# A whole-program order list for a recurrent attention and MLP kernel, and rings of four tiles

## The chip, the cores and the metric

The kernel runs on one NeuronCore of a Trainium2 chip. The metric is device time in microseconds (us) of one execution; the time of a kernel is the median of its runs. A profiled execution has a time of its own and a span, which runs from the first instruction to the end of the last one.

## The reference, cut to what matters

For four batches, eight heads and 768 tokens of head size 48, a recurrent attention gives `y`; the 3072 rows of 384 numbers then go through two matrix products with a leaky ReLU (slope 0.01) between them.

```
for t in range(S):
    cur = einsum('bhd,bhe->bhde', u * k[t], v[t])
    y[t] = einsum('bhd,bhde->bhe', r[t], state + cur)
    state = w * state + einsum('bhd,bhe->bhde', k[t], v[t])
x = y as rows of H * D = 384
h = x @ w_in                 # 384 -> 2048
out = maximum(0.01 * h, h) @ w_out   # 2048 -> 384
```

Inputs and output are float32; the kernel computes mostly in bfloat16.

## The kernel before, in words

The tokens are cut into 24 **stages** of 128 tokens: stage n is chunk n // 4 of batch n % 4, so stage n + 4 goes on from the state that stage n leaves. Each stage is a small chain over five engines, and each step of it has a letter that the program's order list uses, with the stage's number behind it:

- `k`, `r`, `v`: loads of the stage's rows, float32 to bfloat16, as DMAs issued by GpSimd (line 220; 1024 pieces of 192 bytes each). `wi` and `wo` (lines 230 and 234) load quarters of the two weight matrices in the same queue.
- `P` (DVE, line 361): k or r times a table of decay powers. `T` and `t` turn the product so that the head's dimension lies on partitions, by TensorE and a copy (stages 0 to 5); `XT` does the same by a DMA transpose that SyncE issues (line 366, stages 6 to 23).
- `A` (TensorE, line 453): scores of the stage, two PSUM banks. `q` (DVE, lines 390, 392 and 394): row sums of r u k. `Q` (GpSimd, line 401, two instructions): a tile with these sums on its diagonal. `M` (DVE, line 466, two halves `a` and `b`): writes the scores above the diagonal into that tile. Stages 0 to 3 take another way round for the diagonal (`X`, `D`, `Q` on DVE, line 462 for the mask).
- `Y` (TensorE, lines 585 and 592): scores times v plus r times the state. `y` (ScalarE, line 606): copies the result to `xT`.
- `K` (TensorE, line 494) and `S` (DVE, lines 560 and 562, or 557): the new state.
- `G` and `g` (lines 631 and 641): the first product of one stage and a group of 512 of the 2048 columns, and its leaky ReLU on ScalarE into `gT`. `J` and `j` (lines 654 and 664): the same for a pair of stages and 256 columns. A `J` is six matmuls of 256 columns, a `G` twelve of 128.
- `H` and `h` (lines 678 and 690): the second product of one stage, 16 matmuls of 384 columns, its copy and the store, which SyncE issues (line 692).
- `F` with a number: that many matmuls whose results nobody reads.

Every step is recorded by `add` (line 53) with what it reads and writes; each engine then plays its steps strictly in the recorded order, with semaphore waits worked out from the reads and writes. PSUM's eight banks are given out in recorded order too (`take`, line 192). So the order of recording is the order of each engine's queue, and a step that waits holds everything behind it on its engine.

Before, two things set that order. The text `ORDER` (lines 27 to 37) lists the start of the program up to the first matmuls of pair 3. Then a loop (lines 733 to 767) records pair after pair, for m from 3 to 11: the eight `J` of the pair, the scores and masks of the next pair, the preparation (`P`, `XT`) of the pair after, the loads of the one after that, row sums and diagonal tiles, and between them the two `H` of the previous pair and the `Y`, `K` and `S` of the next pair. Up to m = 5 (`LATE`) the scores stand behind the eight `J`; from m = 6 they stand behind the third. Loads in the loop wait for a `J` of the same turn (`pace`, line 753). `xT` and `gT` are rings of three buffers of 256 tokens (line 144).

Of the kernel before, what the change touches and what calls it, by code (L numbers as in the profile page):

```python
# [126 lines left out]
def bass_rwkv5_eagle__then__act_leaky_relu_kernel(  # L127
# [16 lines left out]
    NQK, NTP, NVS, NAT, NT, NX, NG, NO = 6, 6, 6, 6, 10, 3, 3, 4  # L144
# [477 lines left out]
    def g1(n, grp):  # L622
        ps_g, key = g_bank[n, grp] = take()
        m, half = divmod(n, 2)
        ix, t = m % NX, slice(128 * half, 128 * half + 128)

        def emit():
            for f in range(4):
                fb = 4 * grp + f
                for s in range(NSL):  # L630
                    last = PE.matmul(ps_g[:, 128 * f:128 * f + 128], w_in_sb[:, s, 128 * fb:128 * fb + 128],  # L631
                                     xT[ix][:, s, t], start=s == 0, stop=s == NSL - 1)
# [12 lines left out]

    def g1_pair(m, j):
        ps_g, key = g_bank[m, j, 2] = take()
        ix = m % NX

        def emit():  # L650
            for f in range(2):
                fb = 2 * j + f
                for s in range(NSL):
                    last = PE.matmul(ps_g[:, 256 * f:256 * f + 256], w_in_sb[:, s, 128 * fb:128 * fb + 128],  # L654
                                     xT[ix][:, s, :], start=s == 0, stop=s == NSL - 1)
            return last

        add("pe", emit, R=[("xT", ix, 0), ("xT", ix, 1), ("win", j // 2)],
            W=[key, ("pace", 2 * m, j), ("pace", 2 * m + 1, j)])
# [11 lines left out]
    def g2(n, c0=0, c1=HD):  # L671
        ps_o, key = o_bank[n, c0] = take()
        m, half = divmod(n, 2)
        ig = m % NG

        def emit():
            for s in range(NFB):
                last = PE.matmul(ps_o[:, 0:c1 - c0], gT[ig][:, s, 128 * half:128 * half + 128], w_out_sb[:, s, c0:c1],  # L678
                                 start=s == 0, stop=s == NFB - 1)
# [47 lines left out]
    for name in ORDER.split():  # L727
        if name in single:
            single[name]()
        else:  # L730
            what, n, rest = re.match(r"([A-Za-z]+?)(\d+)(.*)$", name).groups()
            stage[what](int(n), rest)
    for m in range(FIRST // 2, NST // 2):
        due, ahead, far = ([n for n in (2 * m + x, 2 * m + x + 1) if n < NST] for x in (2, 4, 6))
        late = m < FIRST // 2 + LATE
        for j in range(8):
            if j == VISIT and not late:
                for n in due:
                    a_mm(n)
            g1_pair(m, j)  # L740
            g1_pair_out(m, j)
        for n in due if late else ():
            a_mm(n)
        if not late:
            for n in ahead:
                prep(n)
        for n in due:
            a_mask(n)
        if late:
            for n in ahead:  # L750
                prep(n)
        for n in far:
            load_stage(n, pace=[("pace", 2 * m, 1)])
        for n in ahead:
            row_sums(n)
            diag_tile(n)
        g2(2 * m - 2)
        g2_out(2 * m - 2)
        for n in due:
            y_part(n)  # L760
        turning = [n for n in due if n < NST - NB]
        for n in turning:
            kv_mm(n)
        for n in turning:
            state(n)
# [64 lines left out]
```

## Time and profile before

| | us |
|---|---|
| median of three runs (lowest, highest) | 169.99 (169.92, 170.53) |
| profiled execution, its time | 170.09 |
| profiled execution, its span | 168.3 |
| TensorE busy in the span | 161.6 |
| GpSimd busy | 111.1 |
| DVE busy | 110.2 |
| ScalarE busy | 91.0 |

The span is 1.79 us shorter than the time of the same execution. Busy times of an engine overlap with those of the others. A matmul's shown duration includes its passage through the array, so of two that follow each other the distance of their starts, and not the duration, is what one costs.

### The profile page before, as it was taken

The numbers are of one execution on the slowest core, as the hardware profiler recorded it, in microseconds if no ns is written. First come the engines' busy times: TensorE is split into PE (matmuls) and PEld (weight loads), VectorE is DVE, ScalarE is ACT, GpSimd is POOL, SyncE is SP. The second block draws the span as 40 slices with busy tenths as digits, with TensorE's granted clock in tenths as the row PEclk, the third lists the DMA queues.
The fourth block names the chain that finished last, engine by engine and source line by source line (L and its number), as shares of the span: only waits on it lengthen the run. The fifth ranks groups of instructions, "written<-read, shape, count | busy, mean of one in ns | idle before, by whom it ended". The sixth has DMA issues, their size and how long they took to land.

```text
span 168.3 us, 4915 instructions
## 1 busy us (share of the span) xinstructions
PE 161.6 (96%) x2116; PEld 122.6 (73%) x2116; DVE 110.2 (66%) x221; ACT 91.0 (54%) x168; POOL 111.1 (66%) x125
## 2 busy tenths in 40 slices
PE   5889979999999999999999999999999999999994
PEld 5767869986568768768668768768678678668663
DVE  7499978828992497497599998996996805000000
ACT  4658777892228537537436536537537447449221
POOL 7999996999699929939939976975960540000000
PEclk9999999999999999999999999999999999999999
DMA  7999999999999996995994995994999111011012
GB/s 108 105 157 162 171 192 167 150 170 155 150 230 150 118 95 186 80 126 156 90 147 129 125 162 142 153 97 113 146 104 143 32 47 51 0 51 47 29 65 95
DMA packets 101263, 20.18 MB, mean 120 GB/s; under 512 B 94457, under 2 KB 101242, under 8 KB 101242
## 3 DMA queue, kind: packets, MB, share of 16 engines
q0 software_dynamic: 76512, 10.03, 93.3%
q1 hardware_dynamic: 23690, 9.64, 28.1%
q8 instruction: 16, 0.26, 0.7%
q10 hardware_dynamic: 1040, 0.20, 0.6%
q14 instruction: 5, 0.04, 0.1%
HBM read 20.45 MB, written 4.72 MB: 150 GB/s over the span
## 4 chain that ended last, share of the span: by engine, by line
PE 69%; POOL 12%; DMA 9%; DVE 7%; issue 1%; ACT 0%; POOLq 0%; DVEq 0%
PE ps L678 31%; PE ps L654 29%; DMA k_sb<-in_k_dram 5%; PE ps L592 5%; DMA r_sb<-in_r_dram 4%; POOL r_sb L220 3%; DVE qk L361 3%; PE ps L453 3%; POOL k_sb L220 3%; POOL v_sb L220 2%; PE ps L494 2%; DVE at L466 1%; POOL at L401 1%; POOL w_in_sb L230 1%; DVE rku L392 1%; DVE ku L390 1%
## 5 line engine op out<-in xcount | busy, mean ns | idle before, releaser
L678 PE MATMUL ps<-w_out_sb,gT 128*128 128x384 bf16 (+2 forms) x400 | 65.6, 320 | 0.0
L401 POOL TENSOR_TENSOR at<-ident,s_tok 128x512 bf16<-128x512 bf16 x40 | 42.8, 1101 | 21.0 <-DVE s_tok L394 21.0
L654 PE MATMUL ps<-xT,w_in_sb 128*128 128x256 bf16 x480 | 54.9, 273 | 0.0
L678 PEld LDWEIGHTS ps<-w_out_sb,gT 128*128 128x128 bf16 x400 | 37.7, 98 | 22.4
L664 ACT ACTIVATE gT<-ps 128x512 bf16<-128x512 f32 x80 | 47.8, 597 | 8.7 <-PE ps L654 4.0
L654 PEld LDWEIGHTS ps<-xT,w_in_sb 128*128 128x128 bf16 x480 | 46.4, 98 | 6.7
L690 ACT ACTIVATE out_sb<-ps 128x384 f32<-128x384 f32 (+2 forms) x25 | 12.0, 479 | 55.8 <-PE ps L678 55.8
L466 DVE CAST_PREDICATED at<-mask,ps 128x512 bf16<-128x512 uint16 x40 | 25.0, 684 | 21.8 <-PE ps L453 21.8
L220 POOL DMA_DIRECT2D k_sb<-in_k_dram x23 | 21.1, 923 | 3.3 <-PE ps L654 3.3
L220 POOL DMA_DIRECT2D v_sb<-in_v_dram x24 | 22.2, 925 | 0.8 <-POOLq L815 0.8
L220 POOL DMA_DIRECT2D r_sb<-in_r_dram x23 | 21.0, 914 | 0.0
L392 DVE TENSOR_TENSOR rku<-r_sb,ku 128x384 bf16<-128x384 bf16 x20 | 17.8, 892 | 0.7
L631 PE MATMUL ps<-xT,w_in_sb 128*128 128x128 bf16 x192 | 12.6, 219 | 0.5 <-DMA w_in_sb<-in_moe_w_in_dram 0.5
L606 ACT ACTIVATE xT<-ps 128x384 bf16<-128x384 f32 x24 | 10.9, 491 | 2.3 <-PE ps L592 2.2
L361 DVE TENSOR_TENSOR qk<-r_sb,qtab 128x384 bf16<-128x384 bf16 x23 | 9.1, 400 | 4.5 <-DMA r_sb<-in_r_dram 4.1
L631 PEld LDWEIGHTS ps<-xT,w_in_sb 128*128 128x128 bf16 x192 | 10.9, 98 | 1.3 <-DMA w_in_sb<-in_moe_w_in_dram 0.7
L394 DVE TENSOR_REDUCE s_tok<-rku 128x8 f32<-128x384 bf16 x20 | 11.1, 553 | 0.7
L641 ACT ACTIVATE gT<-ps 128x512 bf16<-128x512 f32 x16 | 9.5, 599 | 3.4 <-PE ps L631 2.9
L562 DVE TENSOR_TENSOR st<-sum_t,wl 128x384 bf16<-128x384 bf16 x16 | 10.7, 672 | 0.5
L592 PE MATMUL ps<-at,v_sb 128*32 128x128 bf16 x384 | 10.7, 219 | 0.0
L361 DVE TENSOR_TENSOR qk<-k_sb,ktab 128x384 bf16<-128x384 bf16 x23 | 9.9, 434 | 0.7 <-DMA k_sb<-in_k_dram 0.7
L592 PEld LDWEIGHTS ps<-tp,st 128*32 128x32 bf16 x240 | 7.2, 96 | 3.1 <-issue 2.5
(64 smaller groups left out, 120.9 us busy)
## 6 DMA issues: line engine op xcount, KB each, us to landing
out_dram<-out_sb SPq DMA_DIRECT2D x23, 192.0 KB, 2.2
v_sb<-in_v_dram POOLq DMA_DIRECT2D x24, 96.0 KB, 5.3
r_sb<-in_r_dram POOLq DMA_DIRECT2D x23, 96.0 KB, 5.4
k_sb<-in_k_dram POOLq DMA_DIRECT2D x23, 96.0 KB, 5.1
w_in_sb<-in_moe_w_in_dram POOLq DMA_DIRECT2D x4, 384.0 KB, 7.0
w_out_sb<-in_moe_w_out_dram POOLq DMA_DIRECT2D x4, 384.0 KB, 8.5
tp<-qk SPq DMA_TRANSPOSE x18, 4.1
k_f<-in_k_dram ACTq DMA_DIRECT2D x1, 192.0 KB, 2.8
```

The lines of the kernel that those rows point to most:

```text
L220: add("pool", lambda: G.dma_start(dst, src), R=pace, W=[(which, n)], dma=f"{which}{n}")
L361: add("dve", lambda: V.tensor_tensor(qk[iq][:, H * half:H * half + H, 0:D], hd(src), hd(tab[:, :]), ALU.mult), R=[(name, n), "qk"[half] + ...
L392: add("dve", lambda: V.tensor_tensor(rku[i2][:, :], r_of(n), ku[i2][:, :], ALU.mult), R=[("r", n), ("ku", i2)], W=[("rku", i2)])
L394: add("dve", lambda: V.tensor_reduce(s_tok[i2][:, :], hd(rku[i2][:, :]), AX.X, ALU.add), R=[("rku", i2)], W=[("s", i2)])
L401: add("pool", lambda hh=hh, s_of=s_of: G.tensor_tensor(at[ia][:, hh, :, :], ident[:, :].unsqueeze(1).to_broadcast([128, NP, 128]), s_of.un ...
L466: add("dve", lambda: V.copy_predicated(at[n % NAT][:, hh, :, :], mask[:, :].bitcast(mybir.dt.uint16).unsqueeze(1).to_broadcast([128, NP, 1 ...
L592: last = PE.matmul(ps_y[32 * q:32 * q + 32, 128 * s:128 * s + 128], a, m, start=not whole and step == 0, stop=step == len(columns[q]) - 1)
L631: last = PE.matmul(ps_g[:, 128 * f:128 * f + 128], w_in_sb[:, s, 128 * fb:128 * fb + 128], xT[ix][:, s, t], start=s == 0, stop=s == NSL - 1)
L654: last = PE.matmul(ps_g[:, 256 * f:256 * f + 256], w_in_sb[:, s, 128 * fb:128 * fb + 128], xT[ix][:, s, :], start=s == 0, stop=s == NSL - 1)
L664: add("act", lambda: A.activation(gT[ig][:, 2 * j:2 * j + 2, :].rearrange("p f t -> p (f t)"), ps_g[:, :], AF.Prelu, alpha=0.01), R=[key], ...
L678: last = PE.matmul(ps_o[:, 0:c1 - c0], gT[ig][:, s, 128 * half:128 * half + 128], w_out_sb[:, s, c0:c1], start=s == 0, stop=s == NFB - 1)
L690: add("act", lambda: A.activation(out_sb[io][:, c0:c1], ps_o[:, 0:c1 - c0], AF.Copy), R=[key], W=held)
```

## The change

The loop goes. `ORDER` now lists the whole program, stage by stage and engine by engine, in an order that no longer repeats from pair to pair; only the two halves of the last `H` are recorded after it. Every step is there that was there before; the matmuls of `F` come to 49 where they were 55. The loads no longer carry `pace`: their places in GpSimd's queue alone hold them back. `G` and `J` are now one function with a width of one or two stages (a width of four, `Z`, is defined and not used). `xT` and `gT` become rings of two buffers of 512 tokens, so that a place is used again eight stages later instead of six. Below, the new list is cut to the stretches of which the text speaks.

```diff
-FIRST, NB, PACE = 6, B, 3
-TURNED, DIAG, CARRY, EXACT, RAW, VISIT, LATE = 6, 4, 4, 1, 1, 3, 3
+NB = B
+TURNED, DIAG, CARRY, EXACT, RAW = 6, 4, 4, 1, 1
 ORDER = """
-w8 k0 r0 u8 u v0z v0 ones table v0y tcol trow r2 tri id wlz id8 k2 zr F18 Cw c0k Wl wi1 F4 T0k qk0 E r5 c0q F10 T0q wu8
-k1 F1 TQ t0k r1 TK t0q qtab Cu ktab P2q v2 F3 A0 X0 W C P2k T2q k3 M0a D0 T2k t2q Q0 v1 t2k M0b F16 A2 r3 X2 Y0 P1k M2a
-wi3 D2 y0 T1k P1q M2b v3 t1k F3 T1q K2 u16 Q2 G0.1 k5 S2 t1q Y2 g0.1 P3k k4 X1 A1 y2 P5q K1 P3q D1 T3k wi2 M1a T5q t3k
-T3q U t5q@ r4 t3q G2.1 Q1 utab A3 wi0 X3 g2.1 G0.3 M1b wo0 M3b D3 K3 g0.3 Y1 v5 M3a G2.3 y1 Q3 k6 G1.3 P4k g2.3 q5 k7
-Y3 g1.3 T4k y3 v4 G1.1 t4k S3 G3.2 wo1 g1.1 P4q P5k G3.1 Q5 g3.2 S1 T5k g3.1 T4q G3.3 q4 t4q G0.0 t5k r6 g3.3 A4 A5
-g0.0 P0k G3.0 Q4 M5a K0 G1.2 g3.0 M5b S0 K5 G2.2 g1.2 wo3 G2.0 M4a g2.2 wo2 P7k G1.0 g2.0 P6k M4b r7 K4 Y5 g1.0 S4 Y4
-r9 y5 G0.2 S5 y4 k9 J2.7 g0.2 q6 r8 J2.5 j2.7 J2.6 k8 j2.5 J2.4 P6q j2.6 Q6 J2.0 X6T j2.4 J2.1 j2.0 J2.2 j2.1 k10 H2
-j2.2 P7q q7 v6 X7T v7 P9q v8 H3 P9k h2 q9 X9T Q7 P8q H1 h3 Q9 q8 v9 P8k A6 h1 X8T A7 M6b H0 Q8 M6a M7b M7a v11 K7 Y6 h0
-r10 S7 Y7 y6 K6 k11 y7 J2.3 S6 v10 j2.3 r11
+w8 wlz qk0 r0 trow ones F21 k0 table c0k wi1 c0q tcol tri zr id8 Cw F12 k2 id T0k u8 u v0y T0q r2 r1 wu8 v0z Wl E u16
+t0k Cu k1 TQ v0 TK r3 C k3 ktab t0q A0 qtab U utab P2k X0 M0a T2k t2k v2 P2q P1q D0 F4 T2q t2q F12 P1k k5 T1k T1q A2
+t1k wi0 M0b v1 Q0 Y0 P3q X2 D2 t1q A1 M2b T3q P3k T3k M2a y0 G0.1 X1 D1 Q2 Y2 t3q t3k A3 g0.1 W P5k P0k K0 M1a M1b wi2
+T5k Q1 G0.0 S0 y2 G2.0 r5 Y1 y1 M3b v3 K1 S1 g2.0 G2.1 v5 G2.2 g2.1 g2.2 G1.0 g1.0 g0.0 X3 G1.1 g1.1 k4 t5k M3a D3 P5q
+G1.2 r4 wi3 q5 G0.2 Q3 v4 Y3 y3 T5q K5 g1.2 k7 wo3 P4k T4k t4k q4 P4q G3.1 S5 T4q G3.2 wo2 Q5 g0.2 t4q G2.3 g3.1 t5q@
+g2.3 A4 A5 M5a G3.0 r7 Q4 M4a M4b G0.3 g0.3 G3.3 g3.2 K4 wo0 Y4 y4 M5b Y5 G1.3 P7k y5 J2.2 j2.2 J2.7 g3.0 j2.7 q7 K3 S3
+K2 wo1 J2.4 J2.6 S4 r6 k6 S2 P7q X7T r9 k9 P6q P6k r8 J2.0 J2.3 g3.3 q6 P8q v7 q9 r11 k8 j2.3 J2.5 j2.6 j2.4 H0 H3 g1.3
+X6T H2 k11 v6 P9q j2.0 k10 A7 v9 j2.5 A6 Q7 v8 M7a H1 Q6 M6a M6b Y6 M7b r10 P8k y6 r12 P10k P9k v11 q11 Y7 y7 X9T Q9
+q10 h1 h2 J2.1 j2.1 K7 k13 K6 S6 Q10 J3.0 q8 Q8 Q11 P12q v20 P11k h0 J3.5 j3.5 H4 P11q J3.1 j3.1 K8 v12 P10q J3.4 j3.4
+j3.0 X8T H5 v10 S8 S7 A9 M9b r15 X10T X11T A8 h4 h5 J3.2 J3.3 j3.3 J3.7 j3.2 M8a M8b M9a Y8 Y9 A10 A11 k12 y8 M10a M10b
...
+j5.5 J5.0 K13 j5.0 H7 h7 j4.5 P14q k18 P16q P14k j4.2 r20 q12 J5.2 j5.2 J5.7 H6 P17q X12T j4.3 X14T S13 H9 A13 j5.7 A12
+P16k k17 v14 Q13 P17k K14 X17T h6 j5.3 H8 q17 Q14 q15 M13b X16T h9 P15k J5.1 r19 r18 M13a P19k j5.1 P18k Q12 M12a Y13
+M12b P20q y13 Q15 X15T Y12 A14 Q17 q16 M14b v16 P19q X19T r22 A17 y12 J5.6 P18q X18T J6.7 j5.6 v15 r21 J6.0 M14a j6.0
+h8 q19 H10 j6.7 M17a J6.6 S14 q18 A15 Q16 A16 H11 M15a v21 M16b K16 M17b j6.6 M16a M15b k22 K15 h10 Q18 S15 Y17 h11 y17
+Y15 y15 P22q Y14 Y16 S16 A18 M18b y14 A19 J7.2 k20 P22k y16 J8.3 j8.3 J8.4 j8.4 J8.1 J6.2 j6.2 j8.1 J7.0 J7.1 J6.1 J6.3
...
 """
@@
-    NQK, NTP, NVS, NAT, NT, NX, NG, NO = 6, 6, 6, 6, 10, 3, 3, 4
+    NQK, NTP, NVS, NAT, NT, NX, NG, NO = 6, 6, 6, 6, 10, 2, 2, 4
@@
-    xT = [SB(f"xT{i}", [128, NSL, 256]) for i in range(NX)]
-    gT = [SB(f"gT{i}", [128, NFB, 256]) for i in range(NG)]
+    xT = [SB(f"xT{i}", [128, NSL, 512]) for i in range(NX)]
+    gT = [SB(f"gT{i}", [128, NFB, 512]) for i in range(NG)]
@@
-        m, half = divmod(n, 2)
+        ix, slot = n // 4 % NX, n % 4
@@
+    def g1_wide(n0, width, fb0, count):
+        ps_g, key = g_bank[n0, width, fb0] = take()
+        ix, slots = n0 // 4 % NX, range(n0 % 4, n0 % 4 + width)
+        t, step = slice(128 * slots[0], 128 * slots[0] + 128 * width), 128 * width
+
+        def emit():
+            for f in range(count):
+                fb = fb0 + f
                 for s in range(NSL):
+                    last = PE.matmul(ps_g[:, step * f:step * f + step], w_in_sb[:, s, 128 * fb:128 * fb + 128],
                                      xT[ix][:, s, t], start=s == 0, stop=s == NSL - 1)
             return last
@@
-        "G": lambda n, x: g1(n, int(x[1:])), "g": lambda n, x: g1_out(n, int(x[1:])),
-        "J": lambda n, x: g1_pair(n, int(x[1:])), "j": lambda n, x: g1_pair_out(n, int(x[1:])),
+        "G": lambda n, x: g1_wide(n, 1, 4 * int(x[1:]), 4), "g": lambda n, x: g1_wide_out(n, 1, 4 * int(x[1:]), 4),
+        "J": lambda n, x: g1_wide(2 * n, 2, 2 * int(x[1:]), 2), "j": lambda n, x: g1_wide_out(2 * n, 2, 2 * int(x[1:]), 2),
@@
-    for m in range(FIRST // 2, NST // 2):
-        due, ahead, far = ([n for n in (2 * m + x, 2 * m + x + 1) if n < NST] for x in (2, 4, 6))
...
-        g2(2 * m - 1)
-        g2_out(2 * m - 1)
-    g2(NST - 2)
-    g2_out(NST - 2)
+    run(ORDER)
     for c0, c1 in ((0, 256), (256, HD)):
         g2(NST - 1, c0, c1)
         g2_out(NST - 1, c0, c1)
```

More of the change, by code (lines that the diff above doesn't have):

```diff
@@ L646, in g1_pair @@
[L646 to L659, printed above, removed]
@@ L672, in g2 @@
         ps_o, key = o_bank[n, c0] = take()
-        m, half = divmod(n, 2)
-        ig = m % NG
+        ig, slot = n // 4 % NG, n % 4
         def emit():
             for s in range(NFB):
-                last = PE.matmul(ps_o[:, 0:c1 - c0], gT[ig][:, s, 128 * half:128 * half + 128], w_out_sb[:, s, c0:c1],
+                last = PE.matmul(ps_o[:, 0:c1 - c0], gT[ig][:, s, 128 * slot:128 * slot + 128], w_out_sb[:, s, c0:c1],
                                  start=s == 0, stop=s == NFB - 1)
             return last
-        add("pe", emit, R=[("gT", ig, half, j) for j in range(8)] + [("wout", i) for i in range(4)], W=[key])
+        add("pe", emit, R=[("gT", ig, slot, fb) for fb in range(NFB)] + [("wout", i) for i in range(4)], W=[key])
     def g2_out(n, c0=0, c1=HD):
@@ L726, in bass_rwkv5_eagle__then__act_leaky_relu_kernel, with run @@
     }
[L727 to L732, printed above, removed]
-    for m in range(FIRST // 2, NST // 2):
-        due, ahead, far = ([n for n in (2 * m + x, 2 * m + x + 1) if n < NST] for x in (2, 4, 6))
[L735 to L765, printed above, removed]
-        g2(2 * m - 1)
-        g2_out(2 * m - 1)
-    g2(NST - 2)
-    g2_out(NST - 2)
+    def run(names):
+        for name in names.split():
+            if name in single:
+                single[name]()
+            else:
+                what, n, rest = re.match(r"([A-Za-z]+?)(\d+)(.*)$", name).groups()
+                stage[what](int(n), rest)
+    run(ORDER)
     for c0, c1 in ((0, 256), (256, HD)):
```

47 lines of the change are left out of this document (22 added, 25 removed).

## The prediction

> **What bounds the kernel now.** I read the page first, then TensorE's timeline, then the waits, then the timelines of the engines that feed TensorE.
>
> ```profile
> span 168.3 us, 4915 instructions
> PE 161.6 (96%) x2116; PEld 122.6 (73%) x2116; DVE 110.2 (66%) x221; ACT 91.0 (54%) x168; POOL 111.1 (66%) x125
> PE   5889979999999999999999999999999999999994
> ```
>
> TensorE (PE) is busy for 96% of the span, and from the eighth of the 40 slices, some 30 us in, every slice but the last shows a 9. DVE and GpSimd (POOL) are busy for two thirds each. So a new order can save time in the first 30 us alone, and can lose it anywhere. TensorE's timeline gives its prices and the size of the start.
>
> ```profile
> 4.57 0.63 PE L424 MATMUL ps<-ident,raw 128*128 128x128 bf16 x4
> ...
> 29.14 2.17 PE L631 MATMUL ps<-xT,w_in_sb 128*128 128x128 bf16 x36
> 31.15 0.33 PE L494 MATMUL ps<-v_sb,qk 128*128 128x96 bf16 x4
> ...
> 32.99 4.75 PE L654 MATMUL ps<-xT,w_in_sb 128*128 128x256 bf16 x42
> 37.57 7.96 PE L678 MATMUL ps<-w_out_sb,gT 128*128 128x384 bf16 x48
> 45.47 0.82 PE L453 MATMUL ps<-tp 48*128 48x128 bf16 x16
> 46.22 2.77 PE L678 MATMUL ps<-w_out_sb,gT 128*128 128x384 bf16 x16
> ...
> 50.59 6.06 PE L654 MATMUL ps<-xT,w_in_sb 128*128 128x256 bf16 x54
> ...
> 63.69 5.40 PE L654 MATMUL ps<-xT,w_in_sb 128*128 128x256 bf16 x48
> 69.02 0.62 PE L453 MATMUL ps<-tp 48*128 48x128 bf16 x16
> 69.58 2.77 PE L678 MATMUL ps<-w_out_sb,gT 128*128 128x384 bf16 x16
> 72.28 0.24 PE L592 MATMUL ps<-tp,st 128*32 128x128 bf16 x4
> ...
> 73.18 0.51 PE L494 MATMUL ps<-v_sb,qk 128*128 128x96 bf16 x8
> 73.53 2.76 PE L678 MATMUL ps<-w_out_sb,gT 128*128 128x384 bf16 x16
> 76.13 5.40 PE L654 MATMUL ps<-xT,w_in_sb 128*128 128x256 bf16 x48
> ```
>
> From start to start: a G costs 0.67 us ((31.15 - 29.14) / 3), a J 0.67 ((69.02 - 63.69) / 8), an A 0.28 (0.56 / 2), an H 2.63 ((45.47 - 37.57) / 3), a Y 0.45 (0.90 / 2), a K 0.18 (0.35 / 2). A turn of the loop, 63.69 to 76.13, is 12.44 us without a gap. Against that, what stands from 4.57 to 37.57 (16 G, 7 J, six each of A, Y and K, twelve T and small things) comes to some 26 us by such prices and took 33: 7 us of waits and fills.
>
> What keeps the loop free of gaps is slack on the other engines, which the list of waits shows:
>
> ```profile
> DVE at L466 <- PE ps L453: 21.8, 8, 6.4
> POOL at L401 <- DVE s_tok L394: 21.0, 9, 6.5
> ```
>
> DVE waits 21.8 us in all for scores (A), GpSimd 21.0 us for row sums. Both stand ready before TensorE needs them.
>
> **Part 1: the start.** Early on, GpSimd's queue and the transfers set the pace. These are GpSimd's rows around the first two diagonal tiles (Q5, Q4) and behind them, two DMA rows from the chain of waits, the weights' row of the page, and the landing times of the 18 transposes (line 366).
>
> ```profile
> 22.32 2.13 POOL L401 TENSOR_TENSOR at<-ident,s_tok 128x512 bf16<-128x512 bf16 x2
> ...
> 26.75 2.28 POOL L401 TENSOR_TENSOR at<-ident,s_tok 128x512 bf16<-128x512 bf16 x2 [1.47 <-DVE s_tok L394]
> 28.98 1.56 POOL L234 DMA_DIRECT2D w_out_sb<-in_moe_w_out_dram  x2
> 30.53 1.78 POOL L220 DMA_DIRECT2D r_sb<-in_r_dram  x2
> ...
> 15.61 7.52 DMA r_sb<-in_r_dram
> 32.27 8.17 DMA k_sb<-in_k_dram
> w_in_sb<-in_moe_w_in_dram POOLq DMA_DIRECT2D x4, 384.0 KB, 7.0
> DMA to landing us min/median/max: 2.7/4.1/7.4
> ```
>
> r4, issued at 15.61, lands at 23.12; its row sums follow, Q4 starts 1.47 us late and ends at 29.03. Then come two weight quarters and r7, issued at 30.53 and landed near 38.5 (by the 7.5 and 8.2 of the two DMA rows); its transpose takes some 7 us under such load (the 7.4), and the A of stages 6 and 7 stand at 45.47. So that A is Q4's end plus 16.4 us.
>
> The new queue has 23 loads before Q5 where 24 stood. By 0.89 us a row load (1.78 / 2) and 0.78 a weight quarter (1.55 / 2), begun near 1.8 us behind the iotas, Q5 starts near 21.5; r7 follows, and Q4 near 25, once r4 (now the 18th load) and its row sums are there. I take Q4's end at 27.0, 2.0 us earlier; r4's landing, 22 to 24, makes that 26.3 to 28. Behind Q4 stand wo0, wo1, r6 and then k6, one row load more than before ahead of the A: 27.0 + 16.4 + 0.9 gives 44.3 against 45.47, **1.2 us** earlier. TensorE gets there in time. wi0, the tenth load, is issued near 9.7 and lands near 16.5 (the 7.0), and lets G0.0 start. From there 15 G (10.1), Y4 and Y5 (0.9), A4 and A5 (0.6), three K (0.5) and 2.0 for T and the early Y bring the first J to 30.6 (32.99 before); seven J and two K bring the first H to 35.7 (37.57). wo2, issued near 29.8, had landed when that H began; so wo1, issued near 27.8, lands by 35.6. Three H (7.9) end at 43.6, ahead of the A. Then, from 46.22 to 50.59, H0, two Y and two K (3.9) took 4.4 us, for the masks came late; with H1 alone there and the masks straight behind A6 I give back 0.4. **Sum: -1.6 us**, between 0 (r4 as late as before, k6 one load later) and -2.3 (TensorE's own arrival, and the 0.4).
>
> **Part 2: what the lost slack costs.** DVE and GpSimd get in each other's way where a DVE product starts while GpSimd makes a diagonal tile. Two rows of the timelines, then groups and durations (minimum, median, maximum), then DVE undisturbed:
>
> ```profile
> 40.46 2.08 POOL L401 TENSOR_TENSOR at<-ident,s_tok 128x512 bf16<-128x512 bf16 x2
> 40.46 2.30 DVE L361 TENSOR_TENSOR qk<-k_sb,ktab 128x384 bf16<-128x384 bf16 x1 [0.48 <-DMA k_sb<-in_k_dram]
> ...
> L392 DVE TENSOR_TENSOR rku<-r_sb,ku 128x384 bf16<-128x384 bf16 x20 | 17.8, 892 | 0.7
> L392 DVE TENSOR_TENSOR rku<-r_sb,ku x20: 357/358/2905, 20.8 to 132.5; 128x384 bf16<-128x384 bf16 x20
> L562 DVE TENSOR_TENSOR st<-sum_t,wl 128x384 bf16<-128x384 bf16 x16 | 10.7, 672 | 0.5
> L560 DVE TENSOR_TENSOR sum_t<-ps,st 128x384 bf16<-128x384 f32 x16 | 8.8, 548 | 0.7 <-PE ps L494 0.7
> ...
> 57.09 2.48 DVE L466 CAST_PREDICATED at<-mask,ps 128x512 bf16<-128x512 uint16 x4 [5.35 <-PE ps L453]
> 59.49 0.35 DVE L361 TENSOR_TENSOR qk<-r_sb,qtab 128x384 bf16<-128x384 bf16 x1
> 60.56 0.35 DVE L390 TENSOR_TENSOR ku<-k_sb,u_tab 128x384 bf16<-128x384 bf16 x1
> 61.81 0.35 DVE L390 TENSOR_TENSOR ku<-k_sb,u_tab 128x384 bf16<-128x384 bf16 x1
> ```
>
> A product of 0.35 us takes 2.30 when it meets a Q: it ends when both of GpSimd's instructions have ended. The stretch over the run is 20 x (892 - 357) + 16 x (672 - 357) ns = 15.7 us for L392 and L562 (alike in shape); with something for P and ku I take 20 us for 20 diagonal tiles, **1.0 us a tile**. Before, DVE's waits for scores swallowed it. Undisturbed, a half of M costs 0.61 (57.09 to 59.49, by four), a P 0.27 (59.49 to 60.56, by four), a q 1.25 (60.56 to 61.81), an S 0.9 (548 + 357 ns).
>
> The Trainium skill names the cause ("SBUF — State Buffer", Who interferes with whom: a DVE product with two SBUF inputs is fully blocked by a GpSimd instruction that reads SBUF, until that one finishes). By it a block would last one instruction at most, about half my price; the row of 2.30 us, through two instructions, speaks for more.
>
> *Place one, A10 and A11.* From A6 (44.3) TensorE's prices put J3.0 at 49.65, the end of A8 at 58.3, three J, Y8 at 60.3 and A11 at 61.5. On DVE, M7b ends near 46.9; until P10q stand seven P, three q and one S: 6.5 us, 0.5 more for r10's landing, and 3.0 for Q9, Q10 and Q8 beside them. P10q ends near 56.9, X10T goes at once, X11T some 1.3 later, landed near 62.3 (the 4.1). Two S and Q11 (2.8) bring DVE to 59.7, four halves of M to 62.1; so Y8 comes 1.3 late, and A11 near 62.9 instead of 61.5: **+1.4 us**; 0 without the stretch, 4.1 if the transpose takes 7.4.
>
> *Place two, Y17 and Y15.* From the end of A13, TensorE has 14.5 us to Y15: A12, K14, H8, J5.1, Y13, Y12, A14, A17, three J, H10, J6.6, A15, A16, H11, K16, K15, Y17. DVE has from M13b to M15b twelve halves of M (7.4), six P (1.6), three q (3.8), one S (0.9): 13.7 us, 13.9 with two semaphores. Room: 0.6. Q15, Q17 and Q16 fall in that time: 3.0. Also q17, ahead of M13b, waits for k17, the eighteenth load after Q11 (some 16 us of queue), by my sums 0.5 too late for A13. I take **+2.5 us** (rounding 2.9 down, since a Q may fall on masks alone); 0 to 4.
>
> The rest costs nothing in my sum: 49 fills instead of 55 lie where TensorE waits anyway; the rings give room; without `pace` the loads only start earlier. GpSimd's whole work, 111 us, lies ahead of its last use, near 126.
>
> **Sum.** 170.09 - 1.6 + 1.4 + 2.5 = 172.4 for the profiled execution, which is 0.1 over the median of the runs: **172.3 us**.
>
> **The rivals.** *The start's gain stays* (other side: faster). If products and Qs miss each other, both places fit, as the sums without stretch show: 170.0 - 1.6 = 168.4. It decides at about 0.6 us of stretch in place two. For it: after the start the old list had next to no gap, blocks or not. Against: 2.30 for 0.35.
>
> *One place only.* Place one alone gives 169.8, place two alone 170.9.
>
> *The change doesn't do what it says at the start:* r4 and k6 land as late as before, and both places cost: 173.9.
>
> *A cold array.* The first fills run at a slow rate:
>
> ```profile
> 1.33 2.10 PE L267 MATMUL ps<-ones 128*128 128x128 bf16 x18 [1.33 <-DVE ones L257]
> 10.08 1.06 PE L267 MATMUL ps<-ones 128*128 128x128 bf16 x16
> ```
>
> 0.11 us a matmul at first, 0.06 at 10 us. A wait of over 3 us at A11 (the 7.4) might bring the slow rate back for some 3 us, +1.7: 174.0. The Trainium skill ("TensorE: Matmul & The Clock Gate", Part 1) puts the idle window for that at about 3.4 us; the trace shows no return to the slow rate.
>
> **How the numbers follow.** Forecast 0.38 (its own range 170.9 to 174.2), gain kept 0.25, one place 0.20, no gain at the start 0.12, cold array 0.05. Within 0.5% of 169.99 (169.14 to 170.84), about what a measurement tells from no change, lie place one alone and some edges: 0.13. Faster 0.27, slower 0.60. The range, 168.4 to 174.8, leaves out a tenth below (a larger gain) and somewhat less above.
>
> **What would show it.** Q4's end near 27 and the A after the third H near 44.3 bear out part 1. Part 2 holds if TensorE is idle before Y8 and A11 near 60 to 63 us, and before Y17 and Y15 near 97 to 101, with L392's or L562's counterparts stretched beside that of L401. It is wrong if TensorE runs on there, or if it waits for loads, PSUM banks or ScalarE instead.

## The result, and the profile after

The changed kernel takes **181.82 us** (median of 4 runs, 181.01 to 182.62) against 169.95 for the kernel before in the same session: a ratio of 1.069, 95% interval 1.064 to 1.075. The forecast was 172.3, in a range of 168.4 to 174.8: the sign was right, the size far off. Times are medians of all runs of a kernel, while a ratio and its interval leave out runs more than 1.5% above the shortest of the same kernel. The profiled execution took 181.54, its span is 179.6 (168.3 before), so 11.3 us are to be found.

From the page of the changed kernel, the rows that answer to those of before: span, busy times, TensorE's and DVE's slices (4.49 us each), and the granted clock.

```profile
span 179.6 us, 4910 instructions
...
PE 163.9 (91%) x2110; PEld 124.8 (69%) x2110; DVE 114.0 (64%) x221; ACT 84.0 (47%) x168; POOL 111.4 (62%) x125
...
PE   5799989999499869999956998999999999999994
...
DVE  6589998688399973899999999998321800000000
...
PEclk9969999999999999999995699999999999999999
```

Counted from 0, TensorE has holes in slices where it had none before: slice 10 (45 to 49 us), 13 and 14, 20 and 21. The clock row has a 5 and a 6 in slices 21 and 22 (94 to 103 us) where the row of the kernel before is all nines (the 6 in slice 2 lies in the start). And DVE's slices 17 to 26 are all nines. Two windows of both kernels show what that means (columns: PE, PEld, DVE, ACT and POOL busy with their instruction counts, clock, DMA share, GB/s). First the changed kernel, then the one before:

```profile
61.00:75.00 14.00, 11.44 (x227) 9.51 (x227) 9.26 (x20) 7.38 (x15) 14.00 (x17) 1.00 1.88 157
75.00:97.00 22.00, 18.36 (x198) 12.79 (x197) 21.41 (x39) 7.29 (x14) 17.32 (x18) 0.95 1.71 145
```

```profile
75.00:97.00 22.00, 22.00 (x248) 16.47 (x246) 18.57 (x37) 11.88 (x21) 19.15 (x21) 1.00 1.19 131
```

Before, TensorE was busy for all of those 22 us and DVE waited for 3.4 of them. Now DVE works 21.41 of 22 and TensorE waits. What for, says the view of waits by engine (total, times, longest):

```profile
PE ps L470 <- DMA tp<-qk: 4.1, 2, 2.4
PE ps L609 <- DVE at L483: 3.6, 2, 2.3
...
PE ps L648 <- DVE sum_t L577: 1.2, 2, 0.7
...
PE ps L648 <- DVE at L483: 0.3, 2, 0.2
```

L470 is A (it waits for transposes), L609 is Y (it waits for masks), L648 is J, which waits for a PSUM bank that DVE has not read yet. The same waits in order of time, from TensorE's timeline:

```profile
47.95 0.40 PE L470 MATMUL ps<-tp 48*128 48x128 bf16 x8 [2.38 <-DMA tp<-qk]
...
62.33 0.83 PE L648 MATMUL ps<-xT,w_in_sb 128*128 128x256 bf16 x6 [0.72 <-DVE sum_t L577]
63.32 1.48 PE L648 MATMUL ps<-xT,w_in_sb 128*128 128x256 bf16 x12 [0.16 <-DVE at L483]
...
67.74 0.40 PE L470 MATMUL ps<-tp 48*128 48x128 bf16 x8 [1.67 <-DMA tp<-qk]
...
93.10 0.24 PE L609 MATMUL ps<-tp,st 128*32 128x128 bf16 x4 [1.29 <-DVE at L483]
...
96.02 0.30 PE L609 MATMUL ps<-tp,st 128*32 128x128 bf16 x4 [2.35 <-DVE at L483]
...
96.89 1.04 PE L470 MATMUL ps<-tp 48*128 48x128 bf16 x16
97.86 3.98 PE L648 MATMUL ps<-xT,w_in_sb 128*128 128x256 bf16 x18
101.67 1.14 PE L672 MATMUL ps<-w_out_sb,gT 128*128 128x384 bf16 x6
```

In order: A6 waits for X6T, J3.2 for a bank, A11 for X11T, Y13 and Y12 for their masks. Behind the last two the array is slow: 18 matmuls of J take 3.81 us from 97.86 to 101.67, 0.21 each, where the 12 from 63.32 take 0.12 each. That is 1.7 us, and some 0.8 more on Y12, A14 and A17. With 0.67 at J8.3 near 112, the sum is 9.2 of waits and 2.5 of slow clock, 11.7; the first J had come 0.6 earlier than before (32.35 against 32.99), which leaves 11.1 of the 11.3.

The reason for DVE's full slices stands in its own timeline and in GpSimd's:

```profile
79.35 1.47 DVE L378 TENSOR_TENSOR qk<-r_sb,qtab 128x384 bf16<-128x384 bf16 x2
80.74 1.20 DVE L378 TENSOR_TENSOR qk<-k_sb,ktab 128x384 bf16<-128x384 bf16 x1
81.85 1.19 DVE L407 TENSOR_TENSOR ku<-k_sb,u_tab 128x384 bf16<-128x384 bf16 x1
83.08 1.08 DVE L409 TENSOR_TENSOR rku<-r_sb,ku 128x384 bf16<-128x384 bf16 x1
...
85.52 2.49 DVE L579 TENSOR_TENSOR st<-sum_t,wl 128x384 bf16<-128x384 bf16 x1
```

```profile
79.52 4.43 POOL L418 TENSOR_TENSOR at<-ident,s_tok 128x512 bf16<-128x512 bf16 x4 [1.27 <-DVE s_tok L411]
...
85.73 2.06 POOL L418 TENSOR_TENSOR at<-ident,s_tok 128x512 bf16<-128x512 bf16 x2
...
91.19 4.39 POOL L418 TENSOR_TENSOR at<-ident,s_tok 128x512 bf16<-128x512 bf16 x4 [3.40 <-DVE s_tok L411]
```

Four products of 0.35 us take 1.08 to 2.49 beside the first three of these tiles (two instructions each), and a pair takes 1.47. In these rows, products that come directly behind one another pay one after the other, each about until an instruction of GpSimd ends.

### The profile page after: what moved, and what is told of

The parts are those of the page before. It is cut to its first block, busy times and chain, and to the rows that moved or that the text cites. A ratio compares the mean times of both kernels' runs of the same rounds, so it can differ in the third digit from the quotient of the medians.

```text
span 179.6 us, 4910 instructions
## 1 busy us (share of the span) xinstructions
PE 163.9 (91%) x2110; PEld 124.8 (69%) x2110; DVE 114.0 (64%) x221; ACT 84.0 (47%) x168; POOL 111.4 (62%) x125
## 4 chain that ended last, share of the span: by engine, by line
PE 51%; DVE 26%; DMA 15%; POOL 3%; issue 3%; ACT 0%; SPq 0%; DVEq 0%; POOLq 0%
PE ps L648 22%; PE ps L672 20%; DVE qk L378 8%; DMA tp<-qk 8%; DMA r_sb<-in_r_dram 4%; DMA k_sb<-in_k_dram 3%; DVE st L579 3%; DVE ku L407 3%; PE ps L609 3%; DVE at L483 3%; PE ps L470 2%; DVE rku L409 2%; DVE sum_t L577 2%; DVE s_tok L411 2%; PE ps L441 1%
## 5 line engine op out<-in xcount | busy, mean ns | idle before, releaser
L659 ACT ACTIVATE gT<-ps 128x512 bf16<-128x512 f32 x96 | 53.0, 602 | 43.0 <-PE ps L648 42.3
L648 PE MATMUL ps<-xT,w_in_sb 128*128 128x256 bf16 (+1 forms) x672 | 70.5, 261 | 1.6 <-DVE sum_t L577 1.2
L648 PEld LDWEIGHTS ps<-xT,w_in_sb 128*128 128x128 bf16 x672 | 57.3, 99 | 10.3 <-DVE sum_t L577 1.7
L672 PEld LDWEIGHTS ps<-w_out_sb,gT 128*128 128x128 bf16 x400 | 38.2, 98 | 22.7 <-ACT gT L659 0.2
L483 DVE CAST_PREDICATED at<-mask,ps 128x512 bf16<-128x512 uint16 x40 | 25.6, 684 | 10.0 <-PE ps L470 9.9
L684 ACT ACTIVATE out_sb<-ps 128x384 f32<-128x384 f32 (+2 forms) x25 | 11.6, 482 | 21.4 <-PE ps L672 19.2
L623 ACT ACTIVATE xT<-ps 128x384 bf16<-128x384 f32 x24 | 10.9, 493 | 22.5 <-PE ps L609 22.4
L378 DVE TENSOR_TENSOR qk<-r_sb,qtab 128x384 bf16<-128x384 bf16 x23 | 15.8, 700 | 0.8 <-DMA r_sb<-in_r_dram 0.8
L577 DVE TENSOR_TENSOR sum_t<-ps,st 128x384 bf16<-128x384 f32 x16 | 8.8, 551 | 9.2 <-PE ps L511 9.2
L470 PE MATMUL ps<-tp 48*128 48x128 bf16 x192 | 8.6, 225 | 5.1 <-DMA tp<-qk 4.1
L378 DVE TENSOR_TENSOR qk<-k_sb,ktab 128x384 bf16<-128x384 bf16 x23 | 12.4, 556 | 1.3 <-PE ps L511 0.8
L609 PE MATMUL ps<-tp,st 128*32 128x128 bf16 x240 | 9.4, 225 | 3.6 <-DVE at L483 3.6
L407 DVE TENSOR_TENSOR ku<-k_sb,u_tab 128x384 bf16<-128x384 bf16 x20 | 11.8, 590 | 0.0
L411 DVE TENSOR_REDUCE s_tok<-rku 128x8 f32<-128x384 bf16 x20 | 11.1, 553 | 0.8
L470 PEld LDWEIGHTS ps<-tp 48*128 48x128 bf16 x192 | 5.7, 98 | 8.1 <-issue 4.4
L609 PEld LDWEIGHTS ps<-tp,st 128*32 128x32 bf16 x240 | 7.5, 98 | 5.4 <-issue 3.2
L609 PE MATMUL ps<-at,v_sb 128*32 128x128 bf16 x384 | 10.9, 223 | 0.0
```

The costliest lines, as they stand in the source:

```text
L378: add("dve", lambda: V.tensor_tensor(qk[iq][:, H * half:H * half + H, 0:D], hd(src), hd(tab[:, :]), ALU.mult), R=[(name, n), "qk"[half] + ...
L407: add("dve", lambda: V.tensor_tensor(ku[i2][:, :], k_of(n), u_tab[:, :], ALU.mult), R=[("k", n), "u_tab"], W=[("ku", i2)])
L411: add("dve", lambda: V.tensor_reduce(s_tok[i2][:, :], hd(rku[i2][:, :]), AX.X, ALU.add), R=[("rku", i2)], W=[("s", i2)])
L470: last = PE.matmul(at_bank[n][hh][0][:, 128 * p:128 * p + 128], tp[it][rows, NP + p, :], tp[it][rows, p, :], start=True, stop=True)
L483: add("dve", lambda: V.copy_predicated(at[n % NAT][:, hh, :, :], mask[:, :].bitcast(mybir.dt.uint16).unsqueeze(1).to_broadcast([128, NP, 1 ...
L577: add("dve", lambda: V.tensor_tensor(sum_t[n % 4][:, :, :], kv, st[n % NT][:, :, :], ALU.add), R=[key, ("st", n % NT)], W=[("sum", n % 4)])
```

## The experiments

Fifteen kernels ran besides the two. **Theory 1**: the new order leaves DVE no waits to hide the products blocked by GpSimd's tiles (Q), and its first transposes come late. **Rivals**: the start alone, the rings and loads without pace, the clock, the loads' timing.

### Start and rest apart

The order of before with the new start, and the changed program with the start of before:

```diff
 # e1: before.py
-ORDER = (start of before)       + loop of before
+ORDER = (new list, cut to the tokens of that start) + loop of before
 # e2: after.py
-ORDER = (new list)
+ORDER = (start of before) + (the tokens left, in the new list's sequence)
```

> The old loop, rings and pace, behind a start in the new list's order (same steps as the old list, fills of the new one). Theory 1 (products on DVE blocked by diagonal tiles on GpSimd, and transposes that land late, with no slack in the new list): the start keeps its wait before A6, the loop has slack for the rest, so 171 to 172 us (J3.0 came 1.6 us later than before). Rival (the start is good and all the loss lies in the rest): 169.5 to 170. Rival (the loss comes from the new start throwing everything later out of step): 175 or more.

> The old list for the start, then every other step in the new list's order, new rings, no pace. Theory 1: the loss after J3.0 (9.8 of 11.3 us) stays for the most part, 177 to 180 us, with TensorE waiting for masks of stages 12 and 13 and for a transpose at 10 or 11. Rival (the start is at fault): near 170 to 172.

Measured: 173.31 (172.26 to 174.13), ratio 1.019 (1.011 to 1.026), and 185.89 (185.19 to 187.93), ratio 1.095 (1.086 to 1.104). TensorE's waits, first of the new start in the old loop, then of the old start with the new rest:

```profile
PE ps L453 <- DMA tp<-qk: 2.7, 1, 2.7
```

```profile
PE ps L648 <- DVE sum_t L577: 3.8, 2, 3.3
PE ps L609 <- DVE at L483: 3.6, 2, 2.4
```

The new start doesn't gain 1.6 us, it loses 3.3, of which 2.7 are one wait, A6's for X6T. That time lies between the range of the first theory and that of the last rival. The rest loses more without its own start than with it (3.3 us at the bank of one J): the parts don't add, a list is laid for one arrival. That run was 6 us beyond what was expected, and shows only that the rest's waits don't come from the start.

### Rings, pace and program

```diff
-ORDER = (new list)
+ORDER = (list of before) + (its loop, written out)      # after.py otherwise
```

> The changed kernel's program (rings of two tiles of 512 tokens for xT and gT, no paced loads, one function for G and J) with the order of the kernel before, its loop written out. Theory (the order is the whole of the loss): 169.3 to 170.6. Rival (the rings or the loads without pace take part): above 171.5, and waits of ScalarE or TensorE for gT or xT, or of the transposes for earlier loads.

Measured: 169.77 (10 runs, 169.35 to 174.20), ratio 0.999 (0.997 to 1.001). The rings of 512 tokens, the loads without pace and the merged functions cost nothing; the order is the whole of the loss.

### Tiles that read nothing

In both kernels the diagonal tile's product became an iota, an instruction that writes a pattern and reads nothing; these kernels leave out the diagonal part of the scores:

```diff
-add("pool", lambda ...: G.tensor_tensor(at[ia][:, hh, :, :], ident (broadcast), s_of (broadcast), ALU.mult), ...)
+add("pool", lambda hh=hh: G.iota(at[ia][:, hh, :, :], pattern=[[0, NP], [0, 128]], base=0, ...), ...)
```

> The new order with the diagonal tile's two GpSimd instructions replaced by two that write zeros of the same shape and read nothing of SBUF (the diagonal part of the scores is left out); order, waits and DMAs are those of the new kernel. Theory 1: products on DVE no longer stretch, the waits for masks at Y13 and Y12 (3.8 us), the slow clock behind them (2.4) and the waits for banks (2) go, the late transposes stay: 173 to 175 us. Rival (loads and transposes alone set the loss, DVE's stretch is idle time in another place): 179 or more.

> The same replacement in the kernel before (the diagonal part left out), as a control. Theory 1: DVE's stretch was swallowed by its waits, so the time stays within 0.5%, 169.2 to 170.5 us, though products no longer stretch (mean of the L392 group near 360 ns instead of 892).

Measured: the new order 174.08 (171.17 to 176.65), ratio 1.011 (1.001 to 1.021); the old one 169.67 (10 runs, 169.01 to 170.97), ratio 0.999 (0.995 to 1.002). Groups of the old order without reads (the mean in ns ahead of the last bar, then the idle time before them):

```profile
L466 DVE CAST_PREDICATED at<-mask,ps 128x512 bf16<-128x512 uint16 x40 | 25.0, 685 | 32.5 <-PE ps L453 32.5
...
L390 DVE TENSOR_TENSOR ku<-k_sb,u_tab 128x384 bf16<-128x384 bf16 x20 | 7.0, 351 | 0.7 <-DMA k_sb<-in_k_dram 0.7
```

The old order loses 19 us of DVE's work with the blocks (110.2 to 91.2) and gains nothing: its DVE only waits longer for scores, 32.5 us. The new order gains about 8 by the medians, 10 by the ratios. But an iota took 0.597 us and the product 1.10, so GpSimd's shorter work could have helped too. The next run makes the tile as long as it was:

```diff
+add("pool", lambda hh=hh: G.iota(idle[hh][:, :, :], pattern=[[0, NP], [0, 128]], base=0, ...), ...)
 add("pool", lambda hh=hh: G.iota(at[ia][:, hh, :, :], pattern=[[0, NP], [0, 128]], base=0, ...), ...)
```

> The changed kernel with each half of GpSimd's diagonal tile made by two iotas in place of the product of ident and s_tok: as long on GpSimd (about 1.2 us a half by the 0.597 of one iota), but no operand read from SBUF. Left out: the diagonal part of the result (the tiles hold zeros). Theory (DVE is blocked because GpSimd reads SBUF): DVE's products back at 0.36 us and the time 173.0 to 175.5. Rival (what helped without the read was GpSimd's shorter time, 20 us less): DVE's products may be short, but the time is 178 to 182.

Measured: 171.99 (169.57 to 172.33), under the range expected. Its page, the source view of P (minimum, median and maximum in ns), and its waits:

```profile
PE 161.7 (95%) x2110; PEld 124.0 (73%) x2110; DVE 91.5 (54%) x221; ACT 83.8 (49%) x168; POOL 110.5 (65%) x165
```

```profile
L379 DVE TENSOR_TENSOR qk<-r_sb,qtab x23: 347/351/360, 9.9 to 115.0; 128x384 bf16<-128x384 bf16 x23
```

```profile
PE ps L475 <- DMA tp<-qk: 2.1, 1, 2.1
```

In the changed kernel the same group reads:

```profile
L378 DVE TENSOR_TENSOR qk<-r_sb,qtab x23: 343/353/2424, 9.9 to 125.0; 128x384 bf16<-128x384 bf16 x23
```

GpSimd is as busy as in the changed kernel (110.5 against 111.4), writes SBUF no less, and no P takes over 0.36. So it isn't GpSimd's time that costs, but a product with operands from SBUF in place of an instruction without any: **by the medians, 9.8 us of the 11.9 are DVE's blocks**, in this order alone. The four runs scatter by 2.8 us; by the longest and the shortest of them the blocks are worth 9.5 to 12.3. What is left by the medians, 2.0, is about A6's wait of 2.1 in the profiled run (171.80).

### Which tiles

```diff
-"Q": ... diag_tile(n)
+"Q": ... (idle_tile if n < 12 else diag_tile)(n)     # e9; n >= 12 in e10; idle_tile: two iotas a half
```

> The changed kernel with the diagonal tiles of stages 4 to 11 alone made by two iotas a half (as long on GpSimd, no operand read); those of stages 12 to 19 as they are. Left out: the diagonal part of stages 4 to 11. It removes the blocks of the start and of place one. Theory (most of the blocks' price falls in place two, from 75 us on, where DVE is 97% busy): 177.5 to 179.5; A11 then waits for no transpose, for X11T goes before the loads of 61.5 us, but Y13 and Y12 still wait for their masks, 2 us or more. Rival (what is late at place two is only what place one has made late): 172 to 174, with no wait at Y13 and Y12.

> The changed kernel with the diagonal tiles of stages 12 to 19 alone made by two iotas a half; those of stages 4 to 11 as they are. Left out: the diagonal part of stages 12 to 19. Theory (most of the price falls in place two): 174 to 176; the waits at A6 and A11 stay (2.4 and 1.7 us), those at Y13, Y12 and the slow array behind them are gone. Rival (place one decides): 178 to 181, with waits of over 1 us for masks at Y13 and Y12.

Measured: 177.72 (177.07 to 180.52), ratio 1.043 (1.036 to 1.049), and 174.30 (173.96 to 175.96), ratio 1.025 (1.019 to 1.031). The early tiles are worth 4.1 us and the late ones 7.5. First without the early reads, then without the late ones:

```profile
PE ps L623 <- DVE at L497: 3.3, 2, 2.3
...
PE ps L484 <- DMA tp<-qk: 2.1, 1, 2.1
```

```profile
PE ps L484 <- DMA tp<-qk: 4.0, 2, 2.4
```

With the early blocks gone A11's wait goes too, for X11T is issued ahead of the burst of loads; Y13 and Y12 still wait. With the late ones gone only the transposes are left, and 174.30 is 170.46 (before, in that session) plus 3.8, about the 4.0 of those waits. So place two has the larger share, as the theory had it. The two halves together come to 11.6, within what e8 leaves open for the whole (9.5 to 12.3); whether part of the loss needs both isn't shown.

### The slow clock

```diff
-M12a Y13 M12b P20q y13 Q15 X15T Y12 A14
+M12a F16 Y13 M12b P20q y13 Q15 X15T F30 Y12 A14
```

> The changed kernel with 16 fill matmuls ahead of Y13 and 30 ahead of Y12, where TensorE waits 1.29 and 2.35 us for masks; nothing else differs. Theory (the two waits bring the half rate back, and the 0.42 us more of A14 and A17 and the 1.8 us more of the 18 matmuls of J behind them are its price): the granted clock shows no dip in slices 20 and 21, A14 and A17 take 0.62 us, and the time is 179.0 to 180.3. Rival (the slow stretch is not due to idle time, or its price is swallowed by the next wait for a mask or a bank): 181.3 to 182.5.

Measured: 181.06 (180.55 to 181.30), ratio 1.065 (1.062 to 1.068). The clock row, and the waits:

```profile
PEclk9999999999879999999999999999999999999999
```

```profile
PE ps L609 <- DVE at L483: 1.7, 4, 0.7
PE ps L648 <- DVE sum_t L577: 1.1, 1, 1.1
```

The dip at slices 21 and 22 is gone (a slight one in 10 and 11 lies behind A6's wait), so idle TensorE was its cause. But taking away 2.5 us of slow matmuls bought back only 0.8, which the scatter of the runs doesn't tell from nothing (the two intervals overlap): two more Y now wait for masks, and J8.3 waits 1.1 for its bank instead of 0.5. In these rows DVE sets the time. 181.06 lies between the two ranges expected, nearer to the rival's.

### The late transpose

First fewer loads ahead of X6T, in the changed kernel:

```diff
-K4 wo0 ... r6 k6 ... X6T H2 k11 v6 P9q j2.0 k10 A7 v9 j2.5 A6 Q7 v8
+K4 r6 k6 wo0 ... X6T H2 P9q j2.0 A7 j2.5 A6 Q7 v6 k11 k10 v9 v8
```

> The changed kernel with four loads (v6, k11, k10, v9) put behind Q7 on GpSimd's queue, so that they are issued about when the transpose of stage 6 is and not ahead of it, and with r6 and k6 ahead of the weight quarter wo0. Theory (X6T took 8.65 us because it queued behind the loads issued before it): P6q and P6k start some 1.5 us earlier, X6T is issued near 37.6 and lands by 43 to 44.5, A6 waits for nothing, J3.0 starts near 50.5 instead of 52.88; the time is 179.0 to 180.3 if the rest of the list carries that to the end. Rival (DVE and GpSimd set the time from there on, not TensorE): J3.0 early, but the time 181.0 to 182.3. Second rival (a transpose takes its 7 to 9 us whatever loads stand before it): A6 waits as before.

Measured: 181.75 (180.72 to 182.39), ratio 1.069 (1.064 to 1.074). From the chain of the changed kernel the two transfers ahead of A6, the load r6 and the transpose X6T (start, then us to the landing); then the landing times of X7T and X6T here (issued at 36.8 and 38.2), minimum, median and maximum:

```profile
29.68 7.27 DMA r_sb<-in_r_dram
...
39.16 8.65 DMA tp<-qk
```

```profile
DMA to landing us min/median/max: 7.2/8.8/10.3
```

X6T went 1 us earlier, took 10.3 instead of 8.7, and A6 waited until 48.65. X7T lands at 44.0 and X6T 4.5 behind it; in the changed kernel they land at 43.6 and 47.8. The second rival won, as far as fewer loads ahead didn't shorten X6T. Whether the transpose ahead, which was 1.4 us away instead of 2.9, lengthened it isn't shown by this. So X7T was moved, whose P7q stands behind S2 on DVE, though r7 landed long before; and with it wo1, so that r6 and k6 go ahead of it:

```diff
-P7k y5 ... K2 wo1 J2.4 J2.6 S4 r6 k6 S2 P7q X7T r9
+P7k P7q X7T y5 ... K2 J2.4 J2.6 S4 r6 k6 wo1 S2 r9
```

in the kernel without reads (e11), in the new start before the old loop (e12), and in the changed kernel (e13).

> The kernel of two iotas a half (no tile reads; the diagonal part left out) with P7q and X7T moved right behind P7k, and wo1 behind k6 on GpSimd's queue. r7 has landed at 30.5, so X7T can go some 3 us earlier than P7q's place behind S2 lets it, and X6T finds the engines of the DMA with less before it. Theory (A6's wait of 2.1 us is all that is left of the loss without the blocks, and a transpose under load lands 7 us behind its issue or 4 behind the transpose before it): A6 waits under 0.6, and the time is 169.3 to 170.8 against 171.99. Rival (X6T lands late whatever goes before it): A6 waits 1.5 or more and the time stays within 171.3 to 172.5.

> The new start before the old loop (which took 173.31) with P7q and X7T moved right behind P7k, and wo1 behind k6. Theory (of its 3.3 us over the kernel before, 2.7 are A6's wait for X6T): A6 waits under 0.8 and the time is 170.3 to 171.6. Rival: 172.5 to 174.

> The changed kernel with P7q and X7T moved right behind P7k and wo1 behind k6, nothing left out. Theory (from 75 us on DVE, blocked, sets the time; what TensorE gains ahead of that is given back at the next wait for a mask or a bank): A6's wait under 0.8 us, J3.0 near 51, and yet 179.5 to 181.5, so that the 2.4 us of A6's wait are worth under 1.5 as long as the blocks are there. Rival (the waits add up, so that each is worth its own length): 178.6 to 179.4.

Measured: 169.40 (168.55 to 172.15), ratio 0.992 (0.988 to 0.995); 170.70 (169.77 to 173.06), ratio 1.001 (0.997 to 1.004); 182.31 (180.26 to 184.11), ratio 1.075 (1.069 to 1.080). Without blocks and with both moves the new order takes about what the prediction's first rival said, 168.4. In the old loop the two moves take back, by the ratios, nearly all of the start's loss (1.019 to 1.001). In the changed kernel itself it isn't worth what A6 had waited: 182.31 lies above both ranges expected, and can't be told from 181.82. TensorE's timeline of that kernel shows why:

```profile
45.21 0.62 PE L470 MATMUL ps<-tp 48*128 48x128 bf16 x16
...
58.45 0.40 PE L470 MATMUL ps<-tp 48*128 48x128 bf16 x8
59.94 0.40 PE L470 MATMUL ps<-tp 48*128 48x128 bf16 x8 [1.09 <-DVE sum_t L577]
61.06 0.83 PE L648 MATMUL ps<-xT,w_in_sb 128*128 128x256 bf16 x6 [0.72 <-DVE sum_t L577]
```

A7 and A6 run without a wait at 45.21. TensorE comes to A9 2.5 us earlier than in the changed kernel (58.45, there 60.97), but the next one, A8, waits 1.09 for a bank that DVE has not read, and J3.2 starts 1.3 earlier (61.06 for 62.33). Half of the gain is given back to DVE on the spot; the end of this profile, 178.3, keeps the 1.3. The runs scatter by 3.9 us, so that whether even that holds in the median stays open.

In the profile of e12 the first H waited 2.0 us for wo1. That profile is of its run of 173.06, 2.4 us over its median, and no trace shows whether the others had that wait. One more kernel left wo1 in its place:

```diff
-P7k y5 ... S2 P7q X7T r9
+P7k P7q X7T y5 ... S2 r9       # new start before the old loop, as e1
```

> The new start before the old loop with P7q and X7T moved right behind P7k, and wo1 left in its place (with wo1 behind k6 the first H waited 2.0 us for it, and the time was 170.70). Theory (both waits go: wo1 lands near 35, ahead of the first H, and X6T, issued near 37, lands near 45): 168.9 to 170.2, at or just under the kernel before, so that the new start is worth up to 1 us once its transposes are early. Rival (X6T, issued later by the place of r6 and k6, lands near 47, and A6 waits 1.5 us or more): 170.8 to 172.5.

Measured: 172.57 (170.82 to 173.50), ratio 1.012 (1.008 to 1.016). X7T is issued at 31.8, but r6 lands later than in e12, P6q takes 2.25 us, though no Q runs beside it (GpSimd issues loads from 28.2 to 40.2), and X6T is issued at 39.35:

```profile
36.80 2.25 DVE L361 TENSOR_TENSOR qk<-r_sb,qtab 128x384 bf16<-128x384 bf16 x1 [0.82 <-DMA r_sb<-in_r_dram]
...
39.35 7.45 DMA tp<-qk
```

```profile
PE ps L453 <- DMA tp<-qk: 1.3, 1, 1.3
```

A6 waits 1.3 us in a profile (170.82) that is the shortest of its six runs. 172.57 lies just above the rival's range. So an early X7T alone takes the start's ratio from 1.019 to 1.012, which the intervals don't tell apart; the step to 1.001 needed r6 and k6 ahead of wo1 as well. With both moves X6T is issued at 35.5 (e12) and 35.7 (e13) instead of 39.2. And X6T took 7.45 us here, though X7T had landed when it went: by this comparison the transpose ahead is a small part of the 8.65. No version of this start beat the kernel before.

### The tile on another engine

Does the order hold when everything is computed? Eight activations a tile on ScalarE, with e13's early X7T; four idle iotas keep GpSimd's times:

```diff
-add("pool", lambda ...: G.tensor_tensor(at[ia][:, hh, :, :], ident, s_of, ALU.mult))
+add("act", lambda ...: A.activation(at[ia][:, hh, m, :], ident[:, :], AF.Copy, scale=s_tok[n % 4][:, 2 * m + hh:2 * m + hh + 1]))
```

> The whole computation with the new order, the early X7T and the diagonal tiles made by ScalarE: eight activations of 128x128 a tile, ident scaled by one column of s_tok, two at a time between its evictions; GpSimd runs four idle iotas a tile in their place, so that its loads keep their times. Theory (the blocks come from GpSimd's reads, and ScalarE, busy 84 of 180 us, has the room): DVE's products at 0.36 us, ScalarE near 130 us busy, 169.2 to 171.2. Rival (ScalarE's evictions come late by a share of the 2.2 us a tile that the eight take, and TensorE waits for banks and for gT): 172 to 176. Third: a product of DVE is blocked by ScalarE's reads as well: 178 or more.

Measured: 192.49 (191.70 to 195.16), ratio 1.130 (1.126 to 1.134). ScalarE's group, and TensorE's waits, in the profile of its run of 195.16:

```profile
L429 ACT ACTIVATE at<-ident,s_tok 128x128 bf16<-128x128 bf16 x160 | 51.4, 402 | 0.1
```

```profile
PE ps L619 <- DVE at L493: 6.4, 3, 3.9
PE ps L619 <- ACT at L429: 3.3, 1, 3.3
```

DVE's products are at 0.35 again, so ScalarE's reads don't block them. But an activation of 128 columns takes 402 ns, not the 0.28 I had reckoned with; a tile takes 3.2 us, and masks, gT and banks come late by it. That is the rival's mechanism, far beyond its price. No complete kernel without the blocks was found that beats the kernel before.

## Why the prediction was wrong

- **"Q4's end at 27.0 ... the A is Q4's end plus 16.4": failed, in its second half.** Q4 ended at 28.19 (Q5 waited 1.43 for its row sums), 1.2 later than I took. By my own formula the A would stand at 45.5; the second one came at 47.95, at Q4's end plus 19.8. The 16.4 was read from the old list as one piece, and two parts of it were longer in the new one. From the load's landing to the issue of the second transpose it took 2.2 us instead of 0.4 (P6q at 36.98 and P6k at 37.94 were stretched, the rows stand at the end), and that transpose then took 8.65 instead of 7.3. My time for TensorE was early too: it reached the first of the two A at 45.17 without a wait for it, not at 43.6. Instead of -1.6 the start brought +2.0 (e8) to +3.3 (e1). Q4 in the rows:

```profile
26.00 2.19 POOL L418 TENSOR_TENSOR at<-ident,s_tok 128x512 bf16<-128x512 bf16 x2 [0.38 <-DVE s_tok L411]
```

- **"1.0 us a tile": right.** DVE's busy time falls by 22.5 us without reads (114.0 to 91.5), 1.1 a tile for 20 tiles.
- **"Before, DVE's waits for scores swallowed it": right**: e4 without blocks took as long as before.
- **"Place one, A10 and A11: +1.4": the mechanism right, the size not.** A11 waited 1.67 for X11T, which the blocks had pushed into the burst of loads from 61.5 on (e9: the wait gone without blocks). Y8 didn't wait; J3.2 did, for a bank (0.88 with the mask behind it). The early tiles are worth 4.1.
- **"Place two, Y17 and Y15: +2.5 ... Room: 0.6": the step that failed most, a term mis-sized by 5 us.** The late tiles are worth 7.5. I began the sum at A13, with DVE on time, and gave three Qs to the 14.5 us behind it. DVE wasn't on time: from 61 to 75 it waited 4.7 us (busy 9.26 of 14), for scores and for the products of K behind the late A11, and then had 22 us of work without a hole, with five tiles beside it. The rows from 79.35 on alone hold 5.4 us of blocks, most of them ahead of A13 (87.66), where my sum began. The late A11 wasn't needed for that: in e9, where it didn't wait, Y13 and Y12 still waited 3.3 us. So the first to be late were Y13 and Y12 at 93 to 96, ahead of the place that I named.
- **"A cold array ... +1.7", 0.05: present, at another place, and worth less.** It came behind Y13 and Y12, 2.5 us in the profile; taking it away gave 0.8, within the scatter (e5). The Trainium skill ("TensorE: Matmul & The Clock Gate", Part 1) gives about 3.4 us of idle time for the return to half rate; here waits of 1.29 and 2.35 with one short Y between them were enough, while the row shows no dip behind A6's 2.38 alone.
- **"By it a block would last one instruction at most": by the Trainium skill ("SBUF — State Buffer", Who interferes with whom).** The cause it names is borne out: no block where GpSimd's instruction reads nothing (e8, maximum 0.36). The length isn't: 2.42 and 2.49 us are two instructions of 1.09.
- **"The rest costs nothing": right** for rings and pace (169.77).
- **The chances.** "The start's gain stays", 0.25, is about what the order is worth without blocks and with X7T, r6 and k6 early (169.40). The forecast itself added separate terms along TensorE's path, while from 75 us on DVE's was the one that set the end; no rival had that.

## What to carry to other kernels

Before a place is priced alone, carry each engine's lateness into it from the place before: beside an engine at 97% of a window a gain on another engine can be lost (of e13's 2.5 us at A9, 1.2 were gone at J3.2). A stretch that costs nothing in one order (e4) can cost 10 us in another (e8), so the busy time of a slack engine is a debt that a new order may call in.

## What the runs showed of the hardware

- A product of two SBUF operands on DVE (0.35 us) took up to 2.49 beside GpSimd's product of SBUF operands, and never over 0.36 beside iotas of the same total length that only write (e8), or beside ScalarE's activations that read SBUF.
- Two products of P in the changed kernel took 1.03 and 1.19 us, at 36.98 and 37.94, where GpSimd only issued loads; the 2.25 us of e15 had only loads beside it as well. With iotas for the tiles none was stretched there (e8). Why stays open:

```profile
36.98 1.03 DVE L378 TENSOR_TENSOR qk<-r_sb,qtab 128x384 bf16<-128x384 bf16 x1 [0.80 <-DMA r_sb<-in_r_dram]
37.94 1.19 DVE L378 TENSOR_TENSOR qk<-k_sb,ktab 128x384 bf16<-128x384 bf16 x1
```

- Under the loads of the start the second of two transposes landed 4.2 to 4.5 us behind the first, whether issued 2.9 or 1.4 us after it; issued when the first had landed, it still took 7.45 (e15). The shortest of the 18 in the kernel before took 2.7.
- An activation of 128 columns from SBUF took 402 ns (e14), one of 512 columns from PSUM 602: a quarter of the length for two thirds of the time. The two differ in source and function as well, so the part that doesn't depend on the length isn't measured alone.
